# Gated mix of linear and local attention on one core: the first token tile turned by TensorE, its weight pieces all on ScalarE's queue

## The chip, the core and the metric

The kernel runs on one core of one Trainium2 chip. The metric is device time in microseconds (us). Times come in two kinds: plain runs, of which the median counts, and one profiled execution, whose trace gives everything that is said here about single instructions. One core has TensorE (PE; its weight loads are listed apart as PEld), VectorE (DVE), ScalarE (ACT), GpSimd (POOL) and SyncE (SP, which here only issues DMAs). ScalarE issues DMAs too, on a queue of its own. A weight load and a matmul are two instructions, and matmuls write to PSUM, here eight banks of 128 x 512 fp32.

## The reference

Inputs are bf16: tokens x (2048 x 1024), and for each of two blocks A and B a matrix wqkv (1024 x 3072) and wo (1024 x 1024); gate_w has 1024 elements. There are 32 heads of 32.

```python
g = _sigmoid((x * gate_w).sum(-1, keepdims=True))
a = _A_ref(x, A_wqkv, A_wo)   # q, k, v = split(x @ wqkv); phi(t) = (t > 0 ? t + 1 : exp(t)) + 1e-6
                              # o = phi(q) (phi(k)^T v) / (phi(q) . sum phi(k) + 1e-6); o @ wo
b = _B_ref(x, B_wqkv, B_wo)   # token s attends to s, s-2, ..., s-14 (8 positions), softmax; o @ wo
return g * a + (1 - g) * b
```

## The kernel before, in words

Every projection needs x with the model dimension on partitions. The tile xT (128 x 8 x 2048) holds it: slice `xT[:, dc, s]` is the dc-th block of 128 features for token s. It is filled by 16 transposing DMAs, one for each tile of 128 tokens (`load_x`, L1304), all on SyncE's queue.

The work goes in stages on TensorE: the values of B (x @ Wv in two halves of 512 columns, written to a scratch tensor vB in HBM), the gate, the keys and queries of B, A's keys, then the products that A's state is made of, A's queries, and last the two output projections into one PSUM bank. B's attention is spread in slices between the matmuls of the middle stages.

**The order is planned, not written by hand.** `Prog` records operations with engine, a cost, what they read and write, and a priority. `schedule` simulates the engines in time and takes, of the operations that are ready on an engine, the one with the lowest priority value. Each engine then runs its list strictly in that order, with semaphore waits in between. Operations with engine "any" (the copies out of PSUM made by `move`, L1361 and L1362) go to VectorE or ScalarE, whichever the plan thinks will end first. The plan is made up to six times, each time with PSUM banks chosen by what the pass before showed, and the shortest is kept. So an edit at the start can alter the order of copies far behind it.

**The start, which the change is about.** Before any data is there, TensorE runs nine matmuls of 128 x 512 on a zeroed tile `warm` into bank 7 (`WARM`, L1369). VectorE has zeroed `warm` (L1282). The first stage takes token tiles in the order 0 to 3 with the first half of the weights, 0 to 3 with the second half, then 4 to 7, and so on. For each, `group` (L1334) issues eight matmuls of 128 x 512, one per feature block, with the x slice as stationary operand. For tile 0 the group is cut in four pieces of two matmuls, each waiting only for its own piece of weights: a piece is two feature blocks of 512 columns, 256 KB. The first four pieces are issued two on ScalarE's queue and two on SyncE's (`load_w`, L1309):

- SyncE: tile 0 (transposed), weight pieces 3 and 4, tiles 1 to 3 (transposed), the four pieces of the second half, then further tiles mixed with the stores of vB (L1383).
- ScalarE: weight pieces 1 and 2, then the load of its function table, then copies out of PSUM.
- GpSimd: a tile of ones (L1268) and masks for B's attention (L1273 to L1277). VectorE copies the masks (L1279), with waits for GpSimd.

Lines that the steps below name besides: L1435, L1454 and L1460 are B's attention (scores, values, sums), L1441 and L1444 its exponential and mask, L1601 the products for A's state, L1669 the output projection, L1364 its copy out.

Of the kernel before, what the change touches and what calls it, by code (L numbers as in the profile page):

```python
# [7 lines left out]
ALU = mybir.AluOpType  # L8
# [53 lines left out]
class Prog:  # L62
# [16 lines left out]
    def op(self, eng, fn, cost, reads=(), writes=(), prio=None, chan=None, lat=0.0, after=(), name="", mode="m"):  # L79
        o = Op()  # L80
        o.eng, o.fn, o.cost, o.prio, o.chan, o.lat, o.name, o.mode = eng, fn, cost, prio, chan, lat, name, mode
        if prio is None:
            o.prio = 1000 + len(self.ops)
        o.seq = len(self.ops)
        o.deps = set(after)
        o.raw = set(after)
        o.users = []
        rd = [iv for r in reads for iv in r]
        wr = [iv for w in writes for iv in w]
        for sp, lo, hi, own in rd:  # L90
            for rec in self.recs.get(sp, ()):
                if rec[0] < hi and lo < rec[1]:
                    if rec[3]:
                        o.deps.add(rec[2])
                        o.raw.add(rec[2])
                    elif sp == "P" and (rec[2].eng != eng or eng == "any"):
                        o.deps.add(rec[2])
        for sp, lo, hi, own in wr:
            for rec in self.recs.get(sp, ()):
                if rec[0] < hi and lo < rec[1]:  # L100
                    o.deps.add(rec[2])
                    if sp != "P" and rec[4] is not own:
                        o.raw.add(rec[2])
        o.deps.discard(o)
        o.raw.discard(o)
        for sp, lo, hi, own in wr:
            lst = self.recs.setdefault(sp, [])
            lst[:] = [r for r in lst if not (lo <= r[0] and r[1] <= hi)]
            lst.append((lo, hi, o, True, own))
        for sp, lo, hi, own in rd:  # L110
            self.recs.setdefault(sp, []).append((lo, hi, o, False, own))
        for sp, lo, hi, own in rd + wr:
            if sp == "P" and own is not None:
                self.held.setdefault(own, []).append(o)
                if eng != "pe":
                    self.read.add(own)
        self.ops.append(o)
        return o
# [146 lines left out]
class PB:  # L265
# [23 lines left out]
        return list(ws.values())  # L289

    def op(self, eng, fn, waits=(), inc=None, k=1):
        ws = self._merge(eng, waits)

        def thunk(e, fn=fn, ws=ws, inc=inc, k=k):
            for c, v in ws:
                e.wait_ge(c.sem, v)
            ins = fn(e)
            if inc is not None:
                ins.then_inc(inc.sem, k)

        self.progs[eng].append(thunk)
        if inc is not None:
            return inc.bump(k)
        return None
# [798 lines left out]
def build_kernel(nc, A_x, A_wqkv, A_wo, B_x, B_wqkv, B_wo, gate_w, out):  # L1103
# [113 lines left out]

    ph = base[0]
    mx = [SB([128, 1024], BF16, "mx%d" % i, at=ph + 2048 * i) for i in range(2)]
    xn = Ring([SB([128, NT, 256], BF16, "xn%d" % i) for i in range(2)])  # L1220
    top_ = base[0]
    base[0] = ph
# [7 lines left out]
    FILL = 0.2  # L1230
    PVLAG = 3
    SUMS_AT = 2
    WARM = 9
    PASSES = 6
    mm = lambda n: max(n / 2400.0, 0.0267) + 0.0025
    act = lambda n: 0.19 + n / 1200.0
# [2 lines left out]
    def plan(seen):  # L1239
# [25 lines left out]
        def C(eng, fn, cost, writes, reads=()):  # L1265
            return P.op(eng, fn, cost, reads=reads, writes=writes, prio=-1)

        C("pool", lambda e: e.memset(ones[:], 1.0), 0.1, [ones.all()])  # L1268
        for i, (n, offs) in enumerate(KINDS):
            for h, o in enumerate(offs):  # L1270
# [31 lines left out]
        def load_x(t, prio):  # L1302
            e_, r = t // 8, t % 8
            return P.op("sp", lambda e: e.dma_start_transpose(xT[:, :, t * 128:(t + 1) * 128], x2[e_, r * 128:(r + 1) * 128, :]),  # L1304
                        1.5, writes=[xT.part((0, 8), (t * 128, (t + 1) * 128))], prio=prio, chan="x%d" % t, lat=1.3)

        def load_w(slot, half, src, c0, prio, d0=0, d1=8, eng="sp", after=()):
            n = d1 - d0
            return P.op(eng, lambda e: e.dma_start(ws[slot][:, d0:d1, half * 512:half * 512 + 512], src[:, d0:d1, c0:c0 + 512]), 0.4 + 0.2 * n,  # L1309
                        writes=[ws[slot].part((d0, d1), (half * 512, half * 512 + 512))], prio=prio, chan="w%d_%d_%d" % (slot, half, d0), lat=0.55 * n, after=after)  # L1310
# [2 lines left out]
            with nc.allow_non_contiguous_dma(reason="tiny gate_w transposed load"):  # L1313
                return e.dma_start(gw[:, :], gate_w.rearrange("(dc p) -> p dc", p=128))

        load_x(0, 0)
        load_w(0, 0, Bw, 2048, 0.1, 0, 2, "act")
        load_w(0, 0, Bw, 2048, 0.2, 2, 4, "act")
        load_w(0, 0, Bw, 2048, 0.3, 4, 6)
        load_w(0, 0, Bw, 2048, 0.4, 6, 8)  # L1320
        for t in range(1, NT):
            load_x(t, 3 + t)
        for d in range(0, 8, 2):
# [1 line left out]
        P.op("sp", gw_load, 0.6, writes=[gw.all()], prio=20, chan="gw", lat=0.5)  # L1325


        main = Pool(banks[0:7])

        def group(bank, lhs, rhs, reads, lo=0, hi=8):  # L1330
            def fn(e):
                last = None
                for dc in range(lo, hi):
                    last = e.matmul(bank.ap(), lhs(dc), rhs(dc), start=(dc == 0), stop=(dc == 7))  # L1334
                return last
            return P.op("pe", fn, (hi - lo) * mm(512), reads=reads, writes=[bank.iv])
# [28 lines left out]
                fa = lambda e: e.activation(dst, src(), ACT.Copy, scale=scale)  # L1365
            P.op("any", {"act": fa, "dve": fd}, {"act": act(n) + (0.1 if reads else 0.0), "dve": dps(n)}, reads=[bank.iv] + list(reads), writes=[reg])

        for i in range(WARM):
            P.op("pe", lambda e: e.matmul(banks[7].ap(), warm[:, 0:128], warm[:, :], start=True, stop=True), 0.43, reads=[warm.all()], writes=[banks[7].iv], prio=-1)  # L1369
# [407 lines left out]
```

## Time and profile before

| what | us |
|---|---|
| plain runs | 491.48, 492.08, 492.85; median 492.08 |
| profiled execution, its own time | 491.39 |
| its span (first to last instruction) | 489.7 |
| TensorE busy in the span | 474.3 |
| VectorE, ScalarE, GpSimd busy | 277.6, 147.8, 44.2 |
| DMA | 43.25 MB, mean 88 GB/s |

How to read the rows: a row of the timeline or of the table of waits names the engine, the line of the kernel and the operation, then output<-input with their partitions and elements; "x9" is the number of instructions merged in a row; in square brackets stands the idle time of the engine before it, and what ended that idle time. "SPq" and "ACTq" are the times that SyncE and ScalarE take to issue a DMA, not the transfer. A transfer's time runs from issue to landing. A matmul's own duration contains its way through the array, so matmuls overlap, and their pace is read from a stretch divided by their count. The granted clock of TensorE was 0.999 over the span.

### The profile page before, as it was taken

The numbers are of one execution on the slowest core, as the hardware profiler recorded it, in microseconds if no ns is written. First come the engines' busy times: TensorE is split into PE (matmuls) and PEld (weight loads), VectorE is DVE, ScalarE is ACT, GpSimd is POOL, SyncE is SP. The second block draws the span as 40 slices with busy tenths as digits, with TensorE's granted clock in tenths as the row PEclk, the third lists the DMA queues.
The fourth block names the chain that finished last, engine by engine and source line by source line (L and its number), as shares of the span: only waits on it lengthen the run. The fifth ranks groups of instructions, "written<-read, shape, count | busy, mean of one in ns | idle before, by whom it ended". The sixth has DMA issues, their size and how long they took to land.

```text
span 489.7 us, 10830 instructions
## 1 busy us (share of the span) xinstructions
PE 474.3 (97%) x4815; PEld 225.9 (46%) x4878; DVE 277.6 (57%) x457; ACT 147.8 (30%) x229; POOL 44.2 (9%) x43
## 2 busy tenths in 40 slices
PE   7999999999999999999989999999999999999996
PEld 2444444444444444444445455444444444444444
DVE  2112135565677778766742332389987777777522
ACT  2111111111244446666644355444222000011000
POOL 3000000000000000000079931000000000000000
PEclk9999999999999999999999999999999999999999
DMA  8989995000000033113004430252233211132111
GB/s 219 220 206 289 346 332 128 1 0 0 2 24 25 23 112 68 32 33 110 23 25 120 130 101 5 88 173 39 55 80 85 44 43 45 45 79 50 44 44 46
DMA packets 72494, 43.25 MB, mean 88 GB/s; under 512 B 39157, under 2 KB 68214, under 8 KB 72442
## 3 DMA queue, kind: packets, MB, share of 16 engines
q1 hardware_dynamic: 71898, 41.98, 32.1%
q8 instruction: 40, 0.66, 0.6%
q10 hardware_dynamic: 544, 0.52, 0.3%
q14 instruction: 12, 0.10, 0.1%
HBM read 25.70 MB, written 8.40 MB: 70 GB/s over the span
## 4 chain that ended last, share of the span: by engine, by line
PE 95%; issue 2%; DMA 1%; DVE 1%; SPq 0%; ACT 0%
PE ps_all L1334 56%; PE ps_all L1669 23%; PE ps_all L1601 10%; PE ps_all L1435 2%; PE ps_all L1454 2%; DMA xT<-in_A_x_dram 1%; PE ps_all L1460 1%; DVE E L1444 1%; PE ps_all L1580 0%; PE ps_all L1398 0%; ACT E L1441 0%; PE ps_all L1624 0%; SPq L1304 0%; SPq L1309 0%; PE ps_all L1557 0%
## 5 line engine op out<-in xcount | busy, mean ns | idle before, releaser
L1334 PE MATMUL ps_all<-w,xT 128*128 128x512 bf16 x494 | 109.9, 379 | 4.0 <-issue 2.1
L1334 PE MATMUL ps_all<-xT,w 128*128 128x512 bf16 x497 | 109.9, 379 | 1.7 <-issue 1.4
L1334 PEld LDWEIGHTS ps_all<-w,xT 128*128 128x128 bf16 x512 | 48.7, 98 | 60.2 <-issue 1.9
L1334 PEld LDWEIGHTS ps_all<-xT,w 128*128 128x128 bf16 x512 | 49.3, 98 | 58.8 <-issue 0.4
L1340 ACT ACTIVATE e<-ps_all 128x512 bf16<-128x512 f32 x64 | 38.3, 598 | 111.9 <-PE ps_all L1334 110.1
L1669 PE MATMUL ps_all<-kT,aT 128*128 128x512 bf16 (+1 forms) x261 | 60.3, 373 | 0.2
L1669 PE MATMUL ps_all<-w,qT 128*128 128x512 bf16 (+1 forms) x259 | 60.2, 372 | 0.3
L1334 PE MATMUL ps_all<-kT,xT 128*128 128x512 bf16 x248 | 57.1, 379 | 0.6 <-issue 0.3
L1601 PE MATMUL ps_all<-pk,xn 128*128 128x512 bf16 x244 | 55.1, 379 | 1.8 <-issue 1.7
L1669 PEld LDWEIGHTS ps_all<-w,qT 128*128 128x128 bf16 x264 | 25.8, 98 | 29.6
L1669 PEld LDWEIGHTS ps_all<-kT,aT 128*128 128x128 bf16 x264 | 25.8, 98 | 29.4 <-issue 0.2
L1334 PEld LDWEIGHTS ps_all<-kT,xT 128*128 128x128 bf16 x256 | 24.7, 98 | 30.0 <-issue 0.7
L1601 PEld LDWEIGHTS ps_all<-pk,xn 128*128 128x128 bf16 x256 | 24.1, 98 | 27.8
L1364 DVE TENSOR_SCALAR o<-ps_all,gm 128x512 bf16<-128x512 f32 (+1 forms) x27 | 19.7, 731 | 28.2 <-PE ps_all L1669 28.2
L1361 DVE CAST vst<-ps_all 128x512 bf16<-128x512 f32 x15 | 10.4, 692 | 44.4 <-PE ps_all L1334 44.4
L1341 DVE TENSOR_SCALAR e<-e 128x512 bf16<-128x512 bf16 x64 | 18.5, 291 | 28.5 <-ACT e L1340 28.5
L1471 DVE TENSOR_TENSOR qT<-ps_all,L 128x456 bf16<-128x456 f32 (+1 forms) x36 | 21.1, 626 | 23.9 <-ACT L L1470 23.9
L1567 POOL TENSOR_TENSOR zacc<-zacc,pk 128x1024 f32<-128x1024 f32 x15 | 34.5, 2297 | 1.2
L1444 DVE TENSOR_TENSOR E<-E,msk 128x1824 bf16<-128x1824 bf16 (+1 forms) x18 | 22.5, 1250 | 21.1 <-ACT E L1441 21.1
L1441 ACT ACTIVATE E<-ps_all 128x1824 bf16<-128x1824 f32 (+1 forms) x18 | 30.4, 1689 | 12.3 <-PE ps_all L1435 11.5
L1361 DVE CAST kT<-ps_all 128x512 bf16<-128x512 f32 x25 | 17.1, 689 | 24.5 <-PE ps_all L1334 23.8
L1362 ACT ACTIVATE kT<-ps_all 128x512 bf16<-128x512 f32 x23 | 13.2, 598 | 38.4 <-PE ps_all L1334 36.8
(67 smaller groups left out, 332.4 us busy)
## 6 DMA issues: line engine op xcount, KB each, us to landing
v<-vB_hbm SPq DMA_DIRECT2D x36, 128.0 KB, 2.6
vB_hbm<-vst SPq DMA_DIRECT2D x32, 128.0 KB, 4.7
w<-in_B_wqkv_dram SPq DMA_DIRECT2D x4, 1024.0 KB, 8.2
xn<-in_A_x_dram SPq DMA_DIRECT2D x8, 512.0 KB, 5.6
w<-in_A_wqkv_dram SPq DMA_DIRECT2D x4, 1024.0 KB, 9.2
out_dram<-o SPq DMA_DIRECT2D x15, 256.0 KB, 2.1
kT<-in_A_wqkv_dram SPq DMA_DIRECT2D x2, 1024.0 KB, 5.9
kT<-in_A_wo_dram SPq DMA_DIRECT2D x2, 1024.0 KB, 5.4
```

The lines of the kernel that those rows point to most:

```text
L1334: last = e.matmul(bank.ap(), lhs(dc), rhs(dc), start=(dc == 0), stop=(dc == 7))
L1340: P.op("act", lambda e: e.activation(e_[:, :], bank.ap(), ACT.Exp), act(512), reads=[bank.iv], writes=[e_.all()])
L1341: P.op("dve", lambda e: e.tensor_scalar(e_[:, :], e_[:, :], 1.0, 1e-6, op0=ALU.min, op1=ALU.add), 0.25, reads=[e_.all()], writes=[e_.all()])
L1361: fd = lambda e: e.tensor_copy(dst, src())
L1362: fa = lambda e: e.activation(dst, src(), ACT.Copy)
L1364: fd = lambda e: e.tensor_scalar(dst, src(), scale, None, op0=ALU.mult)
L1441: P.op("act", lambda e: e.activation(E[:, 0:32 * nq].rearrange("p (j q) -> p j q", j=4), ps[:, 4:8, 0:8 * nq], ACT.Exp), act(32 * nq), rea ...
L1444: P.op("dve", lambda e: e.tensor_tensor(ev(), ev(), m[:, :, :].rearrange("p r q -> p (r q)")[:, None, :].to_broadcast([128, 16, 2 * nq]), ...
L1471: P.op("dve", lambda e, L=L, pb=pb, g=g: e.tensor_tensor(qT[:, 4 * g:4 * g + 4, t0 + qs:t0 + qs + 2 * nq].rearrange("p c (h q) -> p h c q" ...
L1567: P.op("pool", lambda e, t=t: e.tensor_tensor(zacc[:, :], zacc[:, :], pkS[:, t, :], ALU.add), 2.2, reads=[src, zacc.all()], writes=[zacc.a ...
L1601: last = e.matmul(bank.ap(), tl[:, t, cs:cs + 128], pkS[:, t, r * 512:(r + 1) * 512], start=(t == 0), stop=(t == NT - 1))
L1669: last = e.matmul(bank.ap(0, f1 - f0), lh[:, k, t * 128:(t + 1) * 128], w[:, k, f0:f1], start=(first and k == 0), stop=(not first and k == 7))
```

## The change

Tile 0 is no longer loaded by a transposing DMA. It is loaded plainly, tokens on partitions, into a tile `xf` (128 x 1024), and eight 128 x 128 blocks of it are turned by TensorE with an identity tile that GpSimd makes. The turned blocks stand as bf16 in banks 5 and 6, four in each; VectorE copies the first four into xT, ScalarE the other four. The four first weight pieces are all issued by ScalarE, so that SyncE's queue goes from `xf` straight to tiles 1 to 3 and then to the second half's pieces. Warm-up is seven matmuls ahead of the turn and four behind it. The copies of tile 0 are now dependences by feature block: the first two pairs of matmuls need VectorE's copy, the other two ScalarE's. The first two token tiles use banks 0 to 4, later ones 0 to 6 as before. The edit to `op` in the diff's first hunk belongs to a second code path for other inputs, which these inputs don't take.

```diff
     def op(self, eng, fn, waits=(), inc=None, k=1):
+        if eng == "pool" and inc is not None and k == 1:
+            waits = list(waits) + [(inc, inc.n)]
...
+    xf = SB([128, 1024], BF16, "xf", at=ph + 4096)
+    ident = SB([128, 128], BF16, "ident", at=ph + 6144)
...
-    WARM = 9
+    WARM = 7
...
+        C("pool", lambda e: e.memset(ident[:], 0.0), 0.2, [ident.all()])
+        C("pool", lambda e: e.affine_select(out=ident[:], in_=ident[:], compare_op=ALU.not_equal, fill=1.0, base=0,
+                                            pattern=[[-1, 128]], channel_multiplier=1), 0.3, [ident.all()], [ident.all()])
...
-        load_x(0, 0)
-        load_w(0, 0, Bw, 2048, 0.1, 0, 2, "act")
-        load_w(0, 0, Bw, 2048, 0.2, 2, 4, "act")
-        load_w(0, 0, Bw, 2048, 0.3, 4, 6)
-        load_w(0, 0, Bw, 2048, 0.4, 6, 8)
+        P.op("sp", lambda e: e.dma_start(xf[:, :], x2[0, 0:128, :]), 0.45, writes=[xf.all()], prio=0, chan="xf", lat=0.75)
+        for d in range(0, 8, 2):
+            load_w(0, 0, Bw, 2048, 0.1 + 0.1 * d, d, d + 2, "act")
...
-        main = Pool(banks[0:7])
+        main = Pool(banks[0:5])
...
-        for i in range(WARM):
-            P.op("pe", lambda e: e.matmul(banks[7].ap(), warm[:, 0:128], warm[:, :], start=True, stop=True), 0.43, reads=[warm.all()], writes=[banks[7].iv], prio=-1)
+        def heat(n, prio, after=()):
+            for i in range(n):
+                P.op("pe", lambda e: e.matmul(banks[7].ap(), warm[:, 0:128], warm[:, :], start=True, stop=True), 0.43 if prio == -1 else 0.22,
+                     reads=[warm.all()], writes=[banks[7].iv], prio=prio, after=after)
+
+        heat(WARM, -1)
+        for hf in range(2):
+            b = banks[5 + hf]
+
+            def turn(e, hf=hf, b=b):
+                for i in range(4):
+                    last = e.transpose(b.ap().bitcast(BF16)[:, i * 128:(i + 1) * 128], xf[:, (4 * hf + i) * 128:(4 * hf + i + 1) * 128], ident[:, :])
+                return last
+            o = P.op("pe", turn, 0.3, reads=[xf.all(), ident.all()], writes=[b.iv], prio=-0.5, name="turn")
+            dst = xT[:, 4 * hf:4 * hf + 4, 0:128]
...
+            if hf:
+                P.op("act", lambda e, dst=dst, src=src: e.activation(dst, src(), ACT.Copy), act(512), reads=[b.iv], writes=[reg], prio=3)
+            else:
+                P.op("dve", lambda e, dst=dst, src=src: e.tensor_copy(dst, src()), dps(512), reads=[b.iv], writes=[reg], prio=3)
+        heat(4, -0.4, [o])
...
+            if (t, half) == (2, 0):
+                main = Pool(banks[0:7])
...
-                o = group(bank, xs, w, [xr, ws[0].part((d, d + step), (half * 512, half * 512 + 512))], d, d + step)
+                o = group(bank, xs, w, [xT.part((d, d + step), (t * 128, (t + 1) * 128)), ws[0].part((d, d + step), (half * 512, half * 512 + 512))], d, d + step)
```

More of the change, by code (lines that the diff above doesn't have):

```diff
@@ L1366, in move @@
             P.op("any", {"act": fa, "dve": fd}, {"act": act(n) + (0.1 if reads else 0.0), "dve": dps(n)}, reads=[bank.iv] + list(reads), writes=[reg])
-        for i in range(WARM):
-            P.op("pe", lambda e: e.matmul(banks[7].ap(), warm[:, 0:128], warm[:, :], start=True, stop=True), 0.43, reads=[warm.all()], writes=[banks[7].iv], prio=-1)
+        def heat(n, prio, after=()):
[11 more added lines that the diff above has]
+            dst = xT[:, 4 * hf:4 * hf + 4, 0:128]
+            src = lambda b=b: b.ap().bitcast(BF16)[:, 0:512].rearrange("p (i s) -> p i s", s=128)
+            reg = xT.part((4 * hf, 4 * hf + 4), (0, 128))
+            if hf:
[3 more added lines that the diff above has]
+        heat(4, -0.4, [o])
         early = {(2, 0): (1, 0, Bw, 1024, 21), (4, 1): (2, 0, Bw, 0, 22), (7, 1): (1, 1, Bw, 1536, 23), (10, 1): (2, 1, Bw, 512, 24),
```

## The prediction

> **What bounds the kernel now.** I read the page first: busy time by engine and the chain that ended last.
>
> ```profile
> span 489.7 us, 10830 instructions
> PE 474.3 (97%) x4815; PEld 225.9 (46%) x4878; DVE 277.6 (57%) x457; ACT 147.8 (30%) x229; POOL 44.2 (9%) x43
> PE 95%; issue 2%; DMA 1%; DVE 1%; SPq 0%; ACT 0%
> ```
>
> TensorE is busy for 97% of the span and is 95% of the chain. So the question is where the other 15.4 us (489.7 less 474.3) lie, and which of them the change can reach. The table of waits for TensorE and the last rows of the chain answer that.
>
> ```profile
> PE ps_all L1334 <- issue: 3.8, 24, 0.2
> PE ps_all L1601 <- issue: 1.7, 11, 0.2
> PE ps_all L1334 <- DMA xT<-in_A_x_dram: 1.7, 2, 1.4
> PE ps_all L1369 <- DVE warm L1282: 1.3, 1, 1.3
> PE ps_all L1454 <- DVE E L1444: 1.0, 1, 1.0
> 255.72 0.28 PE ps_all L1454 x24
> 485.50 0.48 DVE o L1364
> ```
>
> The columns are total, times and longest. Some 4.2 us lie behind the last matmul (485.50 to 489.7) and 5.5 us are gaps of 0.2 us at most. The change touches neither. The 1.0 us before L1454 lies at 255 us. What it can reach is the wait for the first tokens, 1.7 us in two pieces, and the stretch before it. TensorE's own timeline shows that stretch:
>
> ```profile
> 1.25 3.50 PE L1369 MATMUL ps_all<-warm 128*128 128x512 bf16 x9 [1.25 <-DVE warm L1282]
> 6.17 1.93 PE L1334 MATMUL ps_all<-w,xT 128*128 128x512 bf16 x8 [1.42 <-DMA xT<-in_A_x_dram]
> 8.33 21.97 PE L1334 MATMUL ps_all<-w,xT 128*128 128x512 bf16 x99 [0.24 <-DMA xT<-in_A_x_dram]
> ```
>
> Nine warm-up matmuls, a wait of 1.42 us, the eight matmuls of tile 0, a wait of 0.24 us, and then no stop. **The number that counts is 8.33**, when tile 1 starts: whatever moves it moves the whole dense rest, and nothing else at the start does. The queues and the landings say what it hangs on:
>
> ```profile
> 0.80 0.94 ACTq L1309 DMA_DIRECT2D w<-in_B_wqkv_dram  x2
> 0.80 1.35 SPq L1304 DMA_TRANSPOSE xT<-in_A_x_dram  x1
> 2.22 1.07 SPq L1309 DMA_DIRECT2D w<-in_B_wqkv_dram  x2
> 3.33 5.13 SPq L1304 DMA_TRANSPOSE xT<-in_A_x_dram  x3
> 2.84 0.45 SPq L1309
> 3.33 4.95 DMA xT<-in_A_x_dram
> DMA to landing us min/median/max: 5.2/5.2/5.2
> L1309 ACTq DMA_DIRECT2D w<-in_B_wqkv_dram x2: 420/454/488, 0.8 to 1.2; - x2
> DMA to landing us min/median/max: 2.8/3.7/4.6
> DMA to landing us min/median/max: 4.6/4.6/4.6
> ```
>
> The landing rows are, in order, tile 0's transpose, the two weight pieces of ScalarE's queue, and the last weight piece of SyncE's. Tile 0 lands at 0.80 + 5.2 = 6.0; the weight pieces at 0.8 + 2.8 = 3.6, 1.2 + 4.6 = 5.8 and (the last, issued at 2.84) 7.4; tile 1, behind them on the same queue, at 3.33 + 4.95 = 8.28. That is the 8.33.
>
> **The change, part by part.** *Removed:* tile 0's transposing DMA, two weight issues on SyncE, and two of nine warm-up matmuls. *Moved:* SyncE issues a plain 256 KB load (0.45 us like one weight issue, against 1.35) and goes straight on to tiles 1, 2 and 3, so tile 1 is issued near 1.3 instead of 3.33. ScalarE issues four weight pieces, done by 0.80 + 4 x 0.47 = 2.7, and then its table load of 1.3 us. *Added:* identity on GpSimd, eight transposing matmuls, one copy on VectorE, one on ScalarE, four warm matmuls behind the transposes.
>
> ```profile
> 0.80 0.20 POOL L1268 MEMSET ones<- 128x128 bf16 x1 [0.29 <-POOLq L1762]
> 1.30 0.55 POOL L1275 TENSOR_SCALAR_AFFINE_SELECT mt<-mt 128x114 bf16<-128x114 bf16 x2
> 1.77 1.28 ACT L1712 ACT_TABLE_LOAD   x1 [1.77 <-PEq L1762]
> 3.36 0.15 PEld L1369 LDWEIGHTS ps_all<-warm 128*128 128x128 bf16 x1 [0.28 <-issue]
> 3.69 0.55 DVE L1279 COPY msk<-mt 64x114 bf16<-64x114 bf16 x2 [1.01 <-POOL mt L1277]
> 3.79 0.15 PEld L1369 LDWEIGHTS ps_all<-warm 128*128 128x128 bf16 x1 [0.28 <-issue]
> 4.16 0.10 PEld L1369 LDWEIGHTS ps_all<-warm 128*128 128x128 bf16 x1 [0.22 <-issue]
> 8.13 0.60 ACT L1362 ACTIVATE vst<-ps_all 128x512 bf16<-128x512 f32 x1 [5.08 <-PE ps_all L1334]
> 12.00 0.69 DVE L1361 CAST vst<-ps_all 128x512 bf16<-128x512 f32 x1 [6.26 <-PE ps_all L1334]
> 15.46 10.74 PE ps_all L1334 x49
> L1334 PE MATMUL ps_all<-w,xT 128*128 128x512 bf16 x494 | 109.9, 379 | 4.0 <-issue 2.1
> L1334 PEld LDWEIGHTS ps_all<-w,xT 128*128 128x128 bf16 x512 | 48.7, 98 | 60.2 <-issue 1.9
> ```
>
> Step by step:
>
> 1. Identity: a memset (0.20) and a select (about 0.3) on GpSimd, ready near 1.9. They push GpSimd's masks back by 0.5 us, so VectorE's mask copy of 3.69 goes at about 4.2 and is done by 4.5, ahead of the copy queued behind it. Hidden.
> 2. Seven warm-up matmuls: the weight loads stand 0.43 apart while they take 0.15 (half clock), so 1.25 + 7 x 0.43 = 4.25. From 4.16 a load takes 0.10: full clock.
> 3. The plain load of tile 0: like a weight piece of the same bytes, 2.8 to 4.6 us from issue, so 3.6 to 5.4. It shares the engines only with the first piece early on; I take 4.2, hidden under step 2. At 5.4 it would cost 1.15.
> 4. Eight transposes, each with its own weights. No row shows one. Below: paced by the weight loads, 8 x 0.098 = 0.8. Above: each pays its whole latency. A 512-column matmul takes 379 ns and the next follows after 10.74 / 49 = 219 ns, so 160 ns lie beyond the pace; with a load (98) and 128 columns (a quarter of 219, 55) that is 0.31 each, 2.5 in all. I take 0.8, since the 98 ns loads of this kernel run ahead of their matmuls. Done at 5.05.
> 5. Copies of 0.69 (VectorE, first half, from about 4.75) and 0.60 (ScalarE, second half, from 5.05; its table load ended near 4.0): ready at 5.45 and 5.65.
> 6. Four warm matmuls at full clock, 4 x 0.22: TensorE is free at 5.92. This is later than both copies, so the copies are hidden and the warm matmuls are the price. Tile 0 starts at 5.92 instead of 6.17, and without a wait ends at 5.92 + 8 x 0.216 = 7.65.
> 7. The last weight piece. Tile 0's last two matmuls need it, 0.43 before the end, so full speed asks for it by 7.2; at 7.9 the gain is gone. Two rows of DMA time bear on it, for 1.8 to 3.3 and 3.3 to 5.1 us (packets, MB, share of 16 engines):
>
> ```profile
> q10 hardware_dynamic: 272, 0.26, 52.2%
> q1 hardware_dynamic: 300, 0.08, 22.4%
> q1 hardware_dynamic: 836, 0.27, 67.3%
> q10 hardware_dynamic: 270, 0.26, 48.0%
> ```
>
> q10 is ScalarE's queue, q1 SyncE's. A weight piece is about 0.48 x 1.8 = 0.86 us of all engines. A transposed tile of 1024 small packets is about 1.35 (q1's 836 packets took 1.21; about 66 of them are larger weight packets). The engines ran at 115%. To finish the plain load (0.86), four pieces (3.46) and tile 1 (1.35) takes 5.67; by 3.3 at least 1.12 is done (74.6% of 1.5 us), and the other 4.55 take 4.0: **7.3, with something for the landing 7.5**. This lets tile 1 go wholly ahead and tile 2 get nothing. Below, pieces alone land 0.8 apart: 6.8. Above, the second piece landed 2.2 behind the first beside a transpose: 4.4 + 3 x 2.2 = 11.0. I take 7.5, the row with both queues in it.
> 8. Tile 1 is then in as well, about 0.8 us ahead of the 8.28 of before, since a 0.86 load replaces a 1.35 one and the queues fill earlier.
>
> Sum: tile 1 starts at 7.5 + 0.43 = 7.95 instead of 8.33: **0.4 us saved**, behind a best of 0.7. Tiles 2 and 3 and the other half's weights stand at the same places behind tile 1 on SyncE's queue and keep the same lead. The planned orders differ further on only in details: the zeroing matmul and one fold stand a group earlier on TensorE, and a few copies change between VectorE and ScalarE (57% and 30% busy). I cost them at nothing; if a copy were late, TensorE would wait some tenths.
>
> The profiled execution took 491.39, 1.7 more than its span; the median of the three runs is 492.08, 0.7 above it. So 491.0 for such an execution and **491.7 for the median**.
>
> **The rivals.**
>
> *The turn is dear and the clock falls (slower).* With step 4 at its upper end the turn ends at 6.75, the warm matmuls at 7.6, tile 0 at 9.35: 1.0 later than 8.33. If TensorE is back at half clock by then, four warm matmuls cost 1.7 and tile 0 3.4: 11.85, or 3.5 later. Median 493.1 to 495.6. It decides at a turn of 1.5 us. For it: the clock had risen only by 4.16, in the seventh to eighth warm matmul, and seven are left. Against it: TensorE stood still for 1.42 us and came back at full clock. [...]
>
> *Weights late (slower, less).* If q1 keeps 67.3 to 48.0 throughout, the pieces left at 3.3 (3.46 less 0.78 of the 52.2%, 2.7) go at 0.48 per us: 8.9, and tile 1 starts 1.0 to 1.2 later than before: 493.2. At the bound of 11.0 it is 3.1 later: 495.2. For it: tiles 1 to 3 now stand beside the pieces; before, two pieces stood ahead of them. It decides at 7.9.
>
> *It comes to nothing.* The last piece and tile 1 still land near 8: 491.9 to 492.4. For it: the same bytes are needed, and DMA is the bound up to there.
>
> *More than that.* The runs lie up to 1.5 above the profiled execution; if they lose that in the landings at the start, the new start may be free of it, and the 1.0 us before L1454 can go when VectorE's operation falls otherwise against GpSimd's. 490.0 to 490.7. Against it: around L1454 only the zeroing matmul moves.
>
> **How the numbers follow.** Forecast (0.3 to 0.7 saved) 0.38; comes to nothing 0.20; weights late 0.17; dear turn 0.12; more 0.13. A difference of 0.3% (1.5 us) is about what a measurement of this kernel can tell from no change. Slower by more: 0.08 of the dear turn and 0.07 of late weights, 0.15. Faster by more: 0.11 of "more" and 0.04 of the forecast by scatter, 0.15. The rest, 0.70, is the same. The range runs from 490.4 to 493.3; it leaves out the half clock, some of the latest weights and the best of "more".
>
> **What would show it.** Right: tile 1 starts at 7.7 to 8.1, no wait for DMA behind it, tile 0 starts near 5.9, weight loads of 0.10 from 4.2 on. Wrong: weight loads of 0.15 behind the transposes (clock); a wait for a weight piece inside tile 0 that ends after 7.9; the load of tile 0 landing after 4.3; a new wait in the middle, or one of 1.0 us gone.

## The result, and the profile after

| | before | changed |
|---|---|---|
| median of 11 plain runs each, us | 491.81 (491.34 to 493.19) | 493.16 (492.32 to 494.30) |
| profiled execution, its own time | 491.39 | 493.02 |
| its span | 489.7 | 491.2 |
| last of the four first weight pieces lands | 7.4 | 8.92 |
| tile 1 starts on TensorE | 8.33 | 9.40 |

The changed kernel is slower by 0.28% (ratio 1.0028, 95% interval 1.0016 to 1.0040). The forecast was 491.7 and tile 1 at 7.95. The time lies inside the range, close to the 493.2 of the rival "weights late".

The page of the changed kernel, with the span, the busy time and the shares of the chain:

```profile
span 491.2 us, 10847 instructions
PE 476.1 (97%) x4825; PEld 227.2 (46%) x4888; DVE 277.7 (57%) x460; ACT 146.5 (30%) x228; POOL 44.6 (9%) x45
PE 95%; issue 2%; DMA 1%; DVE 1%; ACT 0%; ACTq 0%
```

The shares are as before. So the 1.5 us of span are not in the long middle; they must be few and in one place or two. TensorE's timeline from the start shows the place:

```profile
1.25 3.17 PE L1375 MATMUL ps_all<-warm 128*128 128x512 bf16 x7 [1.25 <-DVE warm L1289]
4.70 1.01 PE L1384 MATMUL ps_all<-ident,xf 128*128 128x128 bf16 x8 [0.28 <-POOL mt L1280]
5.50 1.40 PE L1375 MATMUL ps_all<-warm 128*128 128x512 bf16 x4
6.74 1.03 PE L1339 MATMUL ps_all<-w,xT 128*128 128x512 bf16 x4
7.94 0.59 PE L1339 MATMUL ps_all<-w,xT 128*128 128x512 bf16 x2 [0.18 <-DMA w<-in_B_wqkv_dram]
8.97 21.33 PE L1339 MATMUL ps_all<-w,xT 128*128 128x512 bf16 x96 [0.43 <-DMA w<-in_B_wqkv_dram]
```

Before, the eight matmuls of tile 0 were one row without a break, and what followed waited for tile 1. Now tile 0 stands in three rows, and both breaks end with a weight transfer. (The releaser of the row at 4.70 is named as GpSimd's mask; the plain load, issued at 0.80, landed 3.8 later at 4.6, and that is what came last.) The last two matmuls of tile 0 start at 8.97, and tile 1 two matmuls later, 8.97 + 0.43 = 9.40. The chain of waits says the same, and follows the delay down the kernel:

```profile
2.33 6.59 DMA w<-in_B_wqkv_dram
8.97 5.35 PE ps_all L1339 x24
...
128.93 0.63 PE ps_all L1462 x64
...
487.06 0.48 DVE o L1369
```

The chain now starts with ScalarE's queue and its fourth weight piece (2.33 + 6.59 = 8.92), not with SyncE's queue and tile 1. The first group of B's scores stands at 128.93; in the kernel before it stood at 127.87:

```profile
127.87 0.63 PE ps_all L1435 x64
```

That is 1.06 us later, and tile 1 starts **1.07 us** later, so nothing was lost or won between. The last copy out stood at 485.50 and stands at 487.06: 1.56. The other half us is one stop, at 201 us, in the score group's row of the timeline:

```profile
200.43 0.50 PE L1462 MATMUL ps_all<-qT,kT 32*64 32x57 bf16 x40
201.20 0.41 PE L1462 MATMUL ps_all<-qT,kT 32*64 32x57 bf16 x24 [0.27 <-issue]
```

From 200.43 to 201.61 are 1.18 us for 64 matmuls. In another profile of the same kernel (the run "changed again" below) the row is whole:

```profile
200.84 0.70 PE L1462 MATMUL ps_all<-qT,kT 32*64 32x57 bf16 x64
```

So those 0.48 us belong to one execution and not to the change. What the change costs is the 1.07 at the start. In the other profile it is 1.48: there tile 0's last two matmuls start at 9.38 and tile 1 0.43 later, against 8.33.

Where do the pieces lose their time? The queues' issue times, and then the rows of DMA time for 1.8 to 3.3, 3.3 to 5.1 and 5.1 to 8.5 us (packets, MB, share of 16 engines; q10 is ScalarE's queue, q1 SyncE's):

```profile
0.80 2.02 ACTq L1316 DMA_DIRECT2D w<-in_B_wqkv_dram  x4
0.80 0.40 SPq L1323 DMA_DIRECT2D xf<-in_A_x_dram  x1
1.26 7.40 SPq L1311 DMA_TRANSPOSE xT<-in_A_x_dram  x3
```

```profile
q1 hardware_dynamic: 92, 0.18, 78.6%
q10 hardware_dynamic: 17, 0.02, 3.4%
...
q10 hardware_dynamic: 502, 0.49, 78.2%
q1 hardware_dynamic: 223, 0.12, 30.2%
...
q1 hardware_dynamic: 1467, 0.37, 70.3%
q10 hardware_dynamic: 569, 0.54, 57.6%
```

Up to 3.3 us the plain load has the engines nearly to itself: 92 packets, 1.18 us of all engines (78.6% of 1.5), and the weight pieces moved 17 packets. From 3.3 to 5.1 the pieces go fast, 502 packets in 1.8 us. From 5.1 on, SyncE's transposed tiles have more of the engines' time than the pieces, and the 569 weight packets that are left (1088 in all) take until 8.92.

### The profile page after: what moved, and what is told of

It reads as the page before. It is cut to its first block, busy times and chain, and to the rows that moved or that the text cites. A ratio compares the mean times of both kernels' runs of the same rounds, so it can differ in the third digit from the quotient of the medians.

```text
span 491.2 us, 10847 instructions
## 1 busy us (share of the span) xinstructions
PE 476.1 (97%) x4825; PEld 227.2 (46%) x4888; DVE 277.7 (57%) x460; ACT 146.5 (30%) x228; POOL 44.6 (9%) x45
## 3 DMA queue, kind: packets, MB, share of 16 engines
q10 hardware_dynamic: 1088, 1.05, 0.7%
## 4 chain that ended last, share of the span: by engine, by line
PE 95%; issue 2%; DMA 1%; DVE 1%; ACT 0%; ACTq 0%
PE ps_all L1339 56%; PE ps_all L1696 22%; PE ps_all L1628 10%; PE ps_all L1462 2%; PE ps_all L1481 2%; DMA w<-in_B_wqkv_dram 1%; PE ps_all L1487 1%; DVE E L1471 1%; PE ps_all L1607 0%; PE ps_all L1425 0%; ACT E L1468 0%; PE ps_all L1651 0%; ACTq L1316 0%; PE ps_all L1584 0%; DVE o L1369 0%
## 5 line engine op out<-in xcount | busy, mean ns | idle before, releaser
L1297 DVE TENSOR_TENSOR mx<-mx,qT 128x1024 bf16<-128x1024 bf16 x32 | 20.7, 688 | 13.9 <-ACT qT L1370 13.8
L1297 DVE TENSOR_TENSOR mx<-mx,kT 128x1024 bf16<-128x1024 bf16 x32 | 20.7, 687 | 12.0 <-ACT kT L1367 11.9
```

The lines of the kernel that those rows point to most:

```text
L1297: P.op("dve", lambda e, m=m, op=op: e.tensor_tensor(m[:, 0:n], m[:, 0:n], src, op), 0.08 + n / 1920.0, reads=[m.all(), reg], writes=[m.all()],
```

## The experiments

The theory after this reading: **the queue move alone makes the loss; the turn neither gains nor costs.** With all four pieces on ScalarE's queue, SyncE's transposed tiles go out beside pieces 3 and 4 instead of behind them. The rivals: the turn or its second warm-up delays the start; transposing transfers hold up the others in a way that plain ones would not; the time is lost elsewhere. L numbers shift by some lines from kernel to kernel. "Kernel before" means runs on the same chip.

**The turn without the queue move.** Pieces 3 and 4 back on SyncE's queue, behind the plain load:

```diff
-            load_w(0, 0, Bw, 2048, 0.1 + 0.1 * d, d, d + 2, "act")
+            load_w(0, 0, Bw, 2048, 0.1 + 0.1 * d, d, d + 2, "act" if d < 4 else "sp")
```

> The changed kernel with weight pieces 3 and 4 back on SyncE's queue, behind the plain load and ahead of tiles 1 to 3; the turn, its copies and the warm matmuls stay. Theory (weights late: the four pieces share the DMA engines with tiles 1 and 2): the last piece lands near 7 instead of 8.9, tile 1 starts at 8.3 to 8.6 (then set by the turn and the warm matmuls) instead of 9.40, and the time is 0.8 to 1.1 us below the changed kernel's, within 0.3 us of before. Rival (the turn and the warm matmuls are what is dear): tile 1 still starts at 9.2 or later, time 1.0 to 1.4 us above before.

Measured: 491.75 against 491.74, ratio 1.0002 (0.9993 to 1.0010). TensorE's timeline:

```profile
6.14 1.89 PE L1339 MATMUL ps_all<-w,xT 128*128 128x512 bf16 x8
8.20 22.09 PE L1339 MATMUL ps_all<-w,xT 128*128 128x512 bf16 x100 [0.17 <-DMA xT<-in_A_x_dram]
```

Tile 0 is one row again, and tile 1 waits for its own transfer (issued at 2.24, landing 5.92 later at 8.16). The whole turn, warm-up and copies included, costs nothing and gains nothing.

**The queue move without the turn.** The kernel before, with pieces 3 and 4 issued by ScalarE:

```diff
-        load_w(0, 0, Bw, 2048, 0.3, 4, 6)
-        load_w(0, 0, Bw, 2048, 0.4, 6, 8)
+        load_w(0, 0, Bw, 2048, 0.3, 4, 6, "act")
+        load_w(0, 0, Bw, 2048, 0.4, 6, 8, "act")
```

> The kernel before with all four first weight pieces on ScalarE's queue; tile 0 still by transposing DMA, nine warm matmuls, no turn. Theory (weights late): tiles 1 to 3 go ahead of pieces 3 and 4, the last piece lands at 8.5 to 9.3, tile 1 starts at 9.0 to 9.8 instead of 8.33, time 0.7 to 1.4 us above before. Rival (the turn is dear): tile 1 starts within 0.2 of 8.33, time within 0.3 us of before.

Measured: 493.18 (492.59 to 495.80), ratio 1.0037 (1.0021 to 1.0054): the loss of the whole change. First the chain, then TensorE's timeline:

```profile
2.29 7.57 DMA w<-in_B_wqkv_dram
```

```profile
6.28 2.72 PE L1334 MATMUL ps_all<-w,xT 128*128 128x512 bf16 x6 [1.01 <-DMA xT<-in_A_x_dram]
9.91 20.32 PE L1334 MATMUL ps_all<-w,xT 128*128 128x512 bf16 x85 [0.91 <-DMA w<-in_B_wqkv_dram]
```

The last piece lands at 9.86, later than expected (8.5 to 9.3). On a queue of their own the pieces were not spared SyncE's tiles: the fourth was issued earlier (2.29 instead of 2.84) and landed later (9.86 instead of 7.4).

**Without the second warm-up**, once in the changed kernel and once with the pieces two and two:

```diff
-        heat(4, -0.4, [o])
```

> The changed kernel without the four warm matmuls behind the turn. Theory (weights late): tile 0 starts up to 0.8 earlier and then waits longer for the last piece; tile 1 starts at 9.3 to 9.5 as in the changed kernel and the time is within 0.3 us of it, or later by up to 1.7 if TensorE is then still at half clock. Rival (turn and warm matmuls dear): the time falls by 0.9 to 1.2 us.

> Both edits: pieces 3 and 4 on SyncE's queue and no warm matmuls behind the turn. Theory: with the pieces in by about 7, tile 0 is set by the turn alone and tile 1 starts at 7.5 to 8.0 if the clock is full, 8.5 to 9.3 if it is half; time 0.3 to 0.8 us below before in the first case, up to 1 us above it in the second. Rival (turn dear): tile 1 at 8.4 or later, time not below before.

Measured: 493.15 (492.48 to 496.00), ratio 1.0036 (1.0020 to 1.0051), and 491.69, ratio 0.9996 (0.9987 to 1.0006). In the first, tile 0 starts at 5.86 instead of 6.74, and the time saved turns into waiting:

```profile
5.86 1.04 PE L1339 MATMUL ps_all<-w,xT 128*128 128x512 bf16 x4 [0.28 <-DVE xT L1393]
8.48 0.85 PE L1339 MATMUL ps_all<-w,xT 128*128 128x512 bf16 x2 [1.58 <-DMA w<-in_B_wqkv_dram]
9.70 20.55 PE L1339 MATMUL ps_all<-w,xT 128*128 128x512 bf16 x89 [0.37 <-DMA w<-in_B_wqkv_dram]
```

So the second warm-up is no part of the loss. Behind the waits the matmuls of this profile ran with a mean of 529 ns from 9 to 13 us, against 379 over the changed kernel's span: the granted clock was 0.50 from 8.7 to 12.0 us (last section). In the second run the expectation was missed: tile 1 starts at 8.38 and not at 7.5 to 8.0, because its transfer lands at 8.33, and no time is gained.

**Three pieces on ScalarE's queue, one on SyncE's**, with and without the second warm-up:

```diff
-            load_w(0, 0, Bw, 2048, 0.1 + 0.1 * d, d, d + 2, "act")
+            load_w(0, 0, Bw, 2048, 0.1 + 0.1 * d, d, d + 2, "act" if d < 6 else "sp")
```

> The changed kernel with only the fourth weight piece moved to SyncE's queue, behind the plain load and ahead of tile 1; three pieces stay on ScalarE's. Theory (what counts is which transfers stand beside and behind tiles 1 to 3): the last piece lands by 7.5, tile 1 by 7.4 to 8.1, tile 1 starts at 7.9 to 8.3, time from 0.4 us below before to equal to it. Rival (any piece on ScalarE's queue beyond two costs): tile 1 starts near 8.8, halfway between 8.2 and 9.4, time 0.4 to 0.7 us above before.

> The same with the four warm matmuls behind the turn left out. Theory: TensorE reaches tile 0 up to 0.8 earlier but waits for the same transfers; tile 1 starts within 0.3 of the run with the warm matmuls, time within 0.3 us of it, with more scatter because TensorE may fall back to half clock in the gaps. Rival (warm matmuls bound the start): 0.3 to 0.8 us below it.

Measured: 491.91, ratio 1.0002 (0.9993 to 1.0011), and 491.57, ratio 0.9996 (0.9987 to 1.0005). Tile 1's transfer is issued at 1.73 and lands at 8.5 and 8.3; the pieces land later than before (the third at 7.6 in the first). Moving one of the two pieces costs nothing; moving both does.

**Tiles 1 to 3 loaded by plain transfers** in rows of 256 bytes (their transposition is left out), a test of whether transposing as such holds the pieces up:

```diff
+            plain = lambda e: e.dma_start(xT[:, :, t * 128:(t + 1) * 128], x2[e_, r * 128:(r + 1) * 128, :].rearrange("p (d s) -> p d s", s=128))
-            return P.op("sp", lambda e: e.dma_start_transpose(...
+            return P.op("sp", plain if t < 4 else lambda e: e.dma_start_transpose(...
```

> The changed kernel with tiles 1 to 3 loaded by plain DMAs in pieces of 256 bytes instead of transposing ones, in the same place of the queue; this leaves the transposition of three tiles out. Theory (any transfer of these bytes and packets beside the pieces delays them): the last piece still lands at 8.2 to 9.2. Rival (it is the transposing that holds the engines): the last piece lands by 7.5 and tile 1 starts by 8.0.

Measured, one run: 495.57 against 491.65. The chain's transfer:

```profile
2.40 7.97 DMA w<-in_B_wqkv_dram
```

The last piece lands at 10.37, later than beside transposing tiles. (All three tiles are issued by 2.35 here; in the changed kernel the third goes out at 5.76.) That rival falls: it takes no transposition to hold the pieces up; plain packets of 256 bytes do it too.

**Nothing beside the pieces.** SyncE's queue stopped behind the plain load until the fourth piece has landed (`hold` adds a dependence to every later operation of SyncE):

```diff
-            load_w(0, 0, Bw, 2048, 0.1 + 0.1 * d, d, d + 2, "act")
+            last_w = load_w(0, 0, Bw, 2048, 0.1 + 0.1 * d, d, d + 2, "act")
+        P.hold = [last_w]
```

> The changed kernel with SyncE's queue held behind the plain load until the fourth weight piece has landed, so that nothing stands beside the four pieces. Theory: the last piece lands at 6.3 to 7.2 instead of 8.9, tile 0 goes through without a wait of over 0.3 inside it, and tile 1 then starts late, at 9.5 to 11, when its transpose lands. Rival (four pieces on one queue are slow by themselves): the last piece lands at 8.3 or later.

Measured, one run: 494.55 against 491.65. The chain's transfer, and TensorE:

```profile
2.33 4.85 DMA w<-in_B_wqkv_dram
```

```profile
6.90 1.89 PE L1343 MATMUL ps_all<-w,xT 128*128 128x512 bf16 x8
10.76 5.35 PE L1343 MATMUL ps_all<-w,xT 128*128 128x512 bf16 x23 [1.96 <-DMA xT<-in_A_x_dram]
```

The last piece lands at **7.18** instead of 8.92, with the same plain load ahead. Tile 0 runs through; tile 1, issued only at 7.19, is then what is late. Where the difference arises is seen in the DMA time from 5.1 to 6.1 us, first of the changed kernel, then of this run:

```profile
q1 hardware_dynamic: 792, 0.20, 115.9%
q10 hardware_dynamic: 38, 0.03, 9.5%
...
q10 hardware_dynamic: 388, 0.37, 107.5%
```

In the changed kernel the packets of SyncE's queue in this stretch are tile 1's (1024 of 256 bytes start from 4.5 to 6.5 us), and 38 packets of the weights' queue start beside them; with nothing beside them 388 do.

**The changed kernel once more**, without any edit, beside the next kernels:

> The changed kernel once more, unaltered, for a second profile and for times on the chip of the next three. Theory: the last weight piece lands between 8.6 and 9.8, tile 1 starts 0.43 later, the time is 1.0 to 1.8 us above before; the stop of 0.5 us at 201 us in its first profile isn't there again. Rival (that stop belongs to the change): it is there again, and the start explains only 1.1 us.

Measured: 492.49 (492.29 to 493.16), ratio 1.0018 (1.0009 to 1.0027). The last piece lands at 2.32 + 7.01 = 9.33. With the run without the second warm-up (9.65), whose transfers are the same, three profiles give 8.92 to 9.65 for the same transfers; a difference of less than 0.7 between single profiles says nothing.

**Tile 1 ahead of pieces 3 and 4, in the kernel before:**

```diff
-            load_x(t, 3 + t)
+            load_x(t, 3 + t if t > 1 else 0.25)
```

> The kernel before with tile 1's transposing DMA issued on SyncE's queue ahead of weight pieces 3 and 4 instead of behind them; two pieces on each queue, no turn. Theory (what goes ahead of the last piece counts, not which queue issues it): the last piece lands at 8.2 to 9.0, tile 1 starts at 8.7 to 9.4, time 0.3 to 1.0 us above before. Rival (the queue of the issue counts): tile 1 starts within 0.2 of 8.33.

Measured: 491.64 against 491.49, ratio 0.9996 (0.9987 to 1.0006). Tile 1 lands at 6.8, and the last piece at 8.45, as expected. The expected loss of 0.3 to 1.0 us does not show in the interval (0.6 faster to 0.3 slower), though the fastest execution is 0.5 above the fastest of before. The profile can't tell where tile 1 would start: it is of the slowest execution, 493.10, whose weight loads take 0.15 until 10.1 us, most of them 0.43 apart (the one at 8.49, right after a wait, takes 0.10), so that tile 0's slow matmuls hid the wait. One tile ahead of the pieces, with the others behind them, costs at most some tenths.

**The plain load in two halves**, so in rows of 1 KB, each half of the turn waiting for its own; once with the pieces two and two, once with three and one and no second warm-up:

```diff
-        P.op("sp", lambda e: e.dma_start(xf[:, :], x2[0, 0:128, :]), 0.45, writes=[xf.all()], ...
+        for c in (0, 512):
+            P.op("sp", lambda e, c=c: e.dma_start(xf[:, c:c + 512], x2[0, 0:128, c:c + 512]), 0.45, ...
...
-            o = P.op("pe", turn, 0.3, reads=[xf.all(), ident.all()], ...
+            o = P.op("pe", turn, 0.3, reads=[xf.part((512 * hf, 512 * hf + 512)), ident.all()], ...
```

> Two pieces on each queue as in the run that put pieces 3 and 4 back on SyncE's, with tile 0 loaded plainly in two DMAs of 512 columns, so in rows of 1 KB instead of 2 KB. Theory (the plain load in 2 KB rows held the engines for about 1.6 us where a weight piece of the same bytes takes 0.8): both halves are in by 4.2 instead of 4.6, the first weight piece by 4.4 instead of 5.1, tile 1 lands at 7.5 to 7.9 and starts at 7.9 to 8.0; 0.2 to 0.4 us below before. Rival (the bytes bound it): tile 1 lands at 8.0 to 8.3 as in that run, time equal to before.

> The same two half loads with three pieces on ScalarE's queue, the fourth on SyncE's, and no warm matmuls behind the turn. Theory: tile 0 starts near 5.3, the last piece lands by 7.1, tile 1 by 7.9; tile 1 starts at 7.5 to 8.0, time 0.3 to 0.7 us below before. Rival (the bytes bound it): tile 1 starts at 8.2 to 8.6, time equal to before.

Measured: 492.03, ratio 1.0009 (1.0000 to 1.0017), and 491.61, ratio 0.9994 (0.9984 to 1.0004). In the first, the rows of DMA time for 1.8 to 3.3 us:

```profile
q10 hardware_dynamic: 201, 0.20, 43.0%
q1 hardware_dynamic: 149, 0.14, 32.4%
```

The load in two halves lets 201 packets of ScalarE's queue through where 25 went with the whole load and the pieces two and two (17 in the changed kernel), and the first piece lands at 4.1 instead of 5.0. But tile 1 still starts at 8.16, as its transfer lands at 8.11 (2.71 + 5.40), not at 7.5 to 7.9. In the second, tile 1 starts near 7.98, the earliest of all, and 0.25 of it is lost again in a wait for the second half's weights at 15.1 us:

```profile
7.12 7.72 PE L1340 MATMUL ps_all<-w,xT 128*128 128x512 bf16 x34 [0.37 <-DMA w<-in_B_wqkv_dram]
15.08 15.28 PE L1340 MATMUL ps_all<-w,xT 128*128 128x512 bf16 x70 [0.25 <-DMA w<-in_B_wqkv_dram]
```

**Which of SyncE's tiles does it?** The changed kernel with the queue stopped behind tile 1, and behind tile 2 (`t == 2`):

```diff
         for t in range(1, NT):
             load_x(t, 3 + t)
+            if t == 1:
+                P.hold = [last_w]
```

> The changed kernel with SyncE's queue stopped behind tile 1 until the last of ScalarE's four weight pieces has landed, so that tiles 2 and 3 and the second half's pieces start after it. Theory (tile 2's transfer, issued at 2.7 us, takes the engines' time that the last weight piece needs): the last piece lands at 8.4 or before instead of 8.92, tile 0's last two matmuls start by 8.45 and tile 1 by 8.9; tile 2 then lands near 8.4 + 5 = 13, and TensorE waits about 2.5 us for it at 10.6, so the time is about 495 for that reason. Rival (tile 1 alone beside the pieces is enough): last piece at 8.8 to 9.3 as in the changed kernel.

> The changed kernel with SyncE's queue stopped behind tile 2 until the last of the four weight pieces has landed: tiles 1 and 2 go out beside the pieces, tile 3 behind them. Theory (tile 2 is what delays the last piece): last piece at 8.8 to 9.3 as in the changed kernel, tile 1 at about 9.4 to 9.8. If tile 3 too has a part: last piece at 8.5 or before. Tile 3 then lands near 13.5 and is needed at about 12.9: time 493 to 494.

Measured: 493.97, ratio 1.0054 (1.0034 to 1.0074), and 495.08, ratio 1.0089 (1.0056 to 1.0121), both paying for late transfers behind the stop, as they must (the second more than expected: its wait is for the second half's weights, 1.63 us at 18.2). The chain of the first:

```profile
2.33 6.19 DMA w<-in_B_wqkv_dram
```

The last piece lands at 8.52 with tile 1 alone beside it, between what the theory and its rival said, and at 8.83 with tiles 1 and 2. Against 7.18 with nothing beside, tile 1 alone makes 1.3 us. With all three tiles it landed at 8.92, 9.33 and 9.65, so tiles 2 and 3 add another 0.4 to 1.1; with a spread of 0.7 among equal profiles that is not better known.

**The plain load's rows in the changed kernel.** If the 2 KB rows, by estimate 0.8 us of all engines more than rows of 1 KB (1.64 less 0.86), are part of the lateness, halves must bring the last piece forward; the second kernel stops the queue behind tile 1 besides. The edits are those above.

> The changed kernel (four weight pieces on ScalarE's queue), with the plain load cut into two loads of 512 columns, so in rows of 1 KB, and each half of the turn waiting for its own half. Theory (of the prediction's missing 1.4 us in the last piece's landing, about 0.8 is the plain load's rows of 2 KB, which cost 1.6 us of all engines instead of 0.86, and 0.4 is tile 2): the last piece lands near 8.1 to 8.4 instead of 8.9 to 9.3, tile 1 starts near 8.5 to 8.8, time 0.3 to 0.5 above the kernel before. Rival (the plain load's cost is hidden, the pieces are held back only by the transposed tiles): the last piece at 8.9 to 9.3 and the time 1.0 to 1.4 above.

> The same with SyncE's queue stopped behind tile 1 until the last weight piece has landed: the prediction's own picture (tile 1 wholly ahead, tile 2 nothing, a plain load of 0.86 us). Theory: the last piece lands at 7.5 to 7.9. Rival (the plain load's cost is hidden): 8.5 as with the whole load. Tile 2 then comes late, so the time is about 494 in both.

Measured: 493.56 against 491.86, ratio 1.0041 (1.0020 to 1.0061), and 494.36 in one run. The chain of each, first and second:

```profile
2.32 7.36 DMA w<-in_B_wqkv_dram
```

```profile
2.33 6.83 DMA w<-in_B_wqkv_dram
```

The theory falls, and the rival's figures (8.9 to 9.3, and 8.5) are missed too. The third piece comes in at 6.6 and 6.2, so the pieces did start earlier, but the fourth lands at 9.68 and 9.16, no earlier than in the changed kernel. These kernels are not the changed one with a cheaper load and nothing else: the second half's issue pushes tile 1's from 1.26 to 1.73, the third piece now lands ahead of tile 1, and the fourth lands with it (tile 1 at 9.7 and 9.3; in the changed kernel at 7.9, beside the third). The rows of DMA time for 5.1 to 8.5 us of the first:

```profile
q10 hardware_dynamic: 362, 0.35, 60.8%
q1 hardware_dynamic: 1138, 0.29, 53.9%
```

362 weight packets have 60.8% of 3.4 us on 16 engines: 91 ns each. In the changed kernel 569 have 57.6% in that stretch: 55 ns. In the kernel before, from 1.8 to 3.3, 272 packets had 52.2% of 1.5 us: 46 ns. **The time counted for a packet depends on what runs beside it** (and the shares of both queues can add up to more than 100%: 70.3% and 57.6% in the changed kernel); the share of an engine is not a stock of work that can be added up.

## Why the prediction was wrong

It forecast 0.4 us saved; the kernel lost 1.35 by the medians, 1.07 of it in the profile at the place where the gain was looked for. What bounds the kernel was read rightly: tile 1's start carried through to 128 us without change.

1. *Identity hidden*: right. The turn waited for the load, which landed at 4.6.
2. *Warm-up to 4.25*: right, 1.25 + 3.17 = 4.42 to the end of the last one. But what the step calls full clock, weight loads of 0.10, was taken as given from then on, and in the profile it came later, below.
3. *Plain load 0.86 us of all engines, landing at 4.2*: mis-sized. 92 of its 128 packets took 1.18 us, so the load about 1.64 (an estimate); it landed at 4.6 and held the first weight piece back from 3.6 to 5.1. In two halves it doesn't (4.2 beside the same pieces); whether the shorter rows do that or the later issue of the second half was not separated. Nor did the halves bring the fourth piece forward, but they also changed what stood beside it.
4. *Turn 0.8 us, paced by the weight loads*: right. From 4.70 to 5.50, eight transposes, one every 0.1. The first row is of the transposes' own durations (least, median, most):

```profile
L1384 PE MATMUL ps_all<-ident,xf x8: 266/314/314, 4.7 to 5.4; 128*128 128x128 bf16 x8
4.67 0.78 PEld L1384 LDWEIGHTS ps_all<-ident,xf 128*128 128x128 bf16 x8 [1.16 <-POOL mt L1280]
5.32 0.42 DVE L1393 COPY xT<-ps_all 128x512 bf16<-128x512 bf16 x1 [1.00 <-PE ps_all L1384]
5.75 0.60 ACT L1391 ACTIVATE xT<-ps_all 128x512 bf16<-128x512 bf16 x1 [1.62 <-PE ps_all L1384]
5.93 0.15 PEld L1375 LDWEIGHTS ps_all<-warm 128*128 128x128 bf16 x1 [0.28 <-issue]
6.31 0.10 PEld L1375 LDWEIGHTS ps_all<-warm 128*128 128x128 bf16 x1 [0.22 <-issue]
```

   The step's upper end, 0.31 for a transpose, agrees with the duration of a single one here, 266 to 314 ns. But it does not add up to 2.5: eight in a row, each with its own weights, overlap and go through at 0.1 us each. The rival *dear turn* did not come.
5. *Copies hidden*: right. VectorE took 0.42 (0.69 forecast, from a row that read fp32), ScalarE 0.60, done at 5.74 and 6.35, ahead of tile 0 at 6.74.
6. *Four warm matmuls 0.86, tile 0 at 5.92*: wrong by 0.8 in the profile. 0.4 is the late load; the rest is TensorE's pace: the weight load at 5.93 still takes 0.15, and the four took 5.50 to 6.74, 1.24, at a granted clock that reads 1.00. It cost nothing, as the run without them shows: the weights came later still.
7. *The last weight piece at 7.5*: **the step that failed.** It landed at 8.92 (9.33 and 9.65 in other profiles of the same transfers). The step took shares of the DMA engines as work: so much for the load, each piece and tile 1, summed and divided by 115%. Done with the kernel before (tile 0 at 1.35 in place of the load) the same sum (6.16 less 1.12, over 115%, from 3.3 on, and 0.2 for the landing) gives 7.9 for tile 1's landing, where the profile at hand had 8.28. The runs in which SyncE's queue was stopped split what was missing, by one profile each. Without tile 1 the step's sum (4.32 less 1.12, and the rest alike) comes to 6.3; with nothing beside the pieces they land at 7.18. So 0.9 was missing in the load and the pieces themselves; how much of it is the load is open (step 3). With tile 1 alone beside them it is 8.52. That is the step's own picture, and tile 1's packets do go ahead of the third and fourth piece's (in the changed kernel 792 of SyncE's queue against 38 of ScalarE's from 5.1 to 6.1 us): tile 1 adds 1.3, and the step had 1.2 for it, nearly right. Tiles 2 and 3, which the step put at nothing without a reason, add 0.4 to 1.1, though tile 2's transfer goes out at 2.67, long before the pieces land.
8. *Tile 1 0.8 ahead*: its data were, but by 0.4: in at 7.9 instead of 8.28. But TensorE takes tiles in order, and tile 0's last two matmuls stood before it. That order is 0.43 of the 1.07: before, the last of the six transfers to land was tile 1 itself, which started at once; now it is a piece of tile 0's weights, with two matmuls still to run ahead of tile 1. The other 0.64 is 8.28 to 8.92; by the runs with the stopped queue, single profiles again, 0.24 of it is there with tile 1 alone beside the pieces (8.52), and 0.40 comes with tiles 2 and 3.

So the loss against the kernel before and the error of the sum have different parts. The loss comes from moving pieces 3 and 4: the turn without that loses nothing, that without the turn loses as much.

The rival *weights late* named the mechanism, the place and 8.9. Its reckoning was partly luck: it took a steady 0.48 for the pieces from 3.3 on; they had next to nothing until 3.3, 78.2% until 5.1 and 57.6% after that. It deserved more than 0.17: the diff put three transposed tiles beside two pieces that had stood ahead of them, and the profile before already showed the second piece landing 2.2 us behind the first beside one such tile.

Why did no arrangement win? Tile 0, four pieces and tile 1 must all be in before TensorE can run on. The last of the six lands at 8.28 before, 8.16 and 8.33 with the turn and two and two, 8.5 and 8.3 with three and one, 8.45 with tile 1 first, 8.11 and 8.0 with halves: all within 0.2% of before in time. The turn replaced tile 0's transfer, but tile 0 was not what came last. And a second bound stands close behind. In five of these profiles (two and two or three and one, without the second warm-up or with it, and halves with three and one) the chain of waits runs not through tile 1 but through the second half's last weight piece, which lands at 15.0 to 15.5 us (14.7 in the kernel before). The prediction had those weights keep their lead; a tile 1 at 7.95 would have met this bound.

Still open: why the fourth piece is not brought forward when its predecessors are (9.68 and 9.16 with the halves), what makes the 0.9 without any tile, and how much exactly tiles 2 and 3 add to tile 1. Single profiles of equal transfers differ by 0.7 us, so that these runs can't tell.

## What to carry to other kernels

A queue's order acted as a priority here: what stood behind a transfer on its queue hardly competed with it (in the kernel before, 34 of the 456 packets from 5.1 to 6.6 us were under 512 bytes, so tile 1's small packets waited for the pieces ahead of them), and moving the urgent transfers to a queue of their own set the less urgent ones loose beside them. Before moving an issue, list what then goes out beside it, and count the lateness of the last transfer needed, not the earliness of the first. Shares of DMA engines' time from one stretch price packets only for that company (a weight packet had 46, 55 and 91 ns in the three stretches above); the nearest row is one in which the same kinds run side by side.

## What the runs showed of the hardware

**One load in rows of 2 KB held the engines; in two halves, in rows of 1 KB, it did not.** From 1.8 to 3.3 us, 92 packets of the changed kernel's plain load had 1.18 us of 16 engines: 205 ns a packet. Over eight profiles with this load it was 143 to 205 ns, so 72 to 103 for a KB. In the four with the halves a packet of 1 KB had 51 to 78 ns (149 packets, 32.4% of 1.5 us, in the first). ScalarE's queue got 11 to 26 packets through beside the whole load and 149 to 201 beside the halves. The halves are also two DMAs, the second issued 0.46 later; rows and issue were not tried apart.

**When TensorE comes to full speed varies from execution to execution.** Full speed is here a weight load of 0.10 us and a matmul of 379 ns, against 0.15 and 634 in most of the warm-up of the kernel before. By the weight loads in a row without waits, it was there at 4.1 in the kernel before, between 5.9 and 6.3 in the changed one, at 10.5 in the run with tile 1 first and at 13.6 in the queue move alone, here the loads around the turning point, which stand closer from 13.66 on:

```profile
13.30 0.15 PEld L1334 LDWEIGHTS ps_all<-w,xT 128*128 128x128 bf16 x1 [0.28 <-issue]
13.66 0.75 PEld L1334 LDWEIGHTS ps_all<-w,xT 128*128 128x128 bf16 x4 [0.21 <-issue]
```

The granted clock stands at 1.00 in the rows of these stretches (1.2 to 4.2 and 4.2 to 6.2 us of the changed kernel), so only the loads and matmuls show this. In the two latest TensorE stood still for 1.05 and 1.01 us on the way, ahead of tile 0, and in the second of them 0.91 more before 9.91. What sets the turning point was not tested.

Later falls of the clock do show. In the run without the second warm-up, stopped for 1.58 us at 6.9, the stretches 5.3 to 8.6, 8.7 to 12.0 and 12.1 to 15.0 us had granted clocks of 1.00, 0.50 and 1.00; the second is

```profile
8.70:12.00 3.30, 2.93 (x8) 0.89 (x7) 0.00 (x0) 0.60 (x1) 0.00 (x0) 0.50 1.17 276
```

(the granted clock is the third number from the end). In that run the five plain executions of 494.05 us and more, up to 496.00, have mean granted clocks of 0.995 to 0.997, the other seven, up to 493.30, 0.998 to 1.000. So falls of the clock go with most of the scatter of that run. They are not behind that of the kernel before: in the runs beside it, the seven executions above 492.4 have 1.000. What sets a fall off was not tested.
